# Attention and a mixture of experts on one core: experts behind the first taken in the order of their token counts, with 812 to 768 slots by place

## The chip, the core and the metric

The kernel runs on one core of a Trainium2 chip. The metric is the device time of one execution in microseconds (us). PE is the matrix engine (PEld its weight loads), DVE the vector engine, ACT the scalar engine, POOL the third general engine, which also issues the indirect DMAs, and SP the engine that issues the other DMAs.

## The reference

```python
scores = scale * q @ k.T + bias          # 4 x 8 heads, 768 positions, 64 wide, local window of 96 and 8 global keys
x = softmax(scores) @ v                  # as 3072 tokens of 512
noisy = x @ w_gate + log1p(exp(x @ w_noise)) * noise       # 8 experts
top2 = the two largest of noisy for each token, top2_w their softmax
for e in range(8):
    for k in range(2):
        mask = top2[:, k] == e
        out[mask] += top2_w[mask, k] * (relu(x[mask] @ w1[e]) @ w2[e])     # 512 -> 1024 -> 512
```

With the inputs that the reference draws, the eight experts get 721, 802, 751, 806, 768, 763, 761 and 772 tokens.

## The kernel before

The attention runs in 96 head pairs (24 blocks of 128 tokens). Meanwhile `route` places the tokens of five segments of blocks (`SEG`) in a table `tab` of slots: for each expert 7 columns, 4 of 128 slots (part A, `CA` = 512) and 3 of 100 (part B, `CB` = 300), so `CAP` = 812 for every expert. It is a Python generator: each `yield` is one step, and its caller decides how many steps are written between other work. Its last part makes, for each block, two marks on DVE (L350, L354: tiles `m` and `xg`), and L367 multiplies them on PE into `tab`, in groups of at most three blocks. Instructions run on each engine in the order in which they are written.

The experts come one after another. Their weights are loaded by SP in halves of 1 MB into a ring of three buffers (`load_w`, L130) and each value is split into a high and a low part (`split`: ACT L141, DVE L142). Tokens are gathered by slot (`gather`, L158), transposed on PE (`turn`, L180) and split (ACT L182, DVE L183). `up` multiplies by `w1` for one of 8 pieces `f`, 12 matmuls of 512 columns (part A, c=0) or 300 (part B, c=1), L781; ACT L785 and DVE L786 take the result. `down` (part A, L808) yields a tile of tokens from 24 matmuls of 512 columns. `down_t` (part B, L818) multiplies the other way round, 24 matmuls with the 300 slots as columns, and `back` (L828) transposes its result. `put` scales (ACT L792) and adds the rows into the output by an indirect DMA (POOL L793); its tile `y` has two buffers.

Between the attention and expert 0's first `up`, two routes are unfinished. They are handed to `pending`, and this list says how many steps of each are written ahead of each `up(0, 0, f)`:

```python
steps_of = [24, 0, 8, 100], [0, 25, 0, 0, 0, 26]
```

A branch behind the end computes all experts densely for tokens beyond the slots; it is not entered when no expert has more tokens than `CAP`.

Of the kernel before, what the change touches and what calls it, by code (L numbers as in the profile page):

```python
# [10 lines left out]
F32 = mybir.dt.float32  # L11
# [12 lines left out]
TB, MB = 3, 100  # L24
CA, CB = TA * P, TB * MB
TT = TA + TB
CAP = CA + CB
DUMP = 512


# [1 line left out]
def tile_local_global_attention_then_moe(  # L32
# [13 lines left out]
    nc = tc.nc  # L46
    B, _, _, D, _, HP, Q = q.shape
    H = 2 * HP
    Dm = H * D
# [3 lines left out]
    E, _, F = w1.shape  # L53
    KC, FC = Dm // P, F // P
# [18 lines left out]
    gp = wctx.enter_context(tc.tile_pool(name="gp", bufs=1))  # L73
# [15 lines left out]
    ident = consts.tile([P, P], F32, name="ident")  # L89
# [5 lines left out]
    iota_e = consts.tile([P, SW, E], F32, name="iota_e")  # L95
    carry = consts.tile([P, E], F32, name="carry")
# [17 lines left out]
    raw = {}  # L114
    order = [(x, e, h) for e in range(E) for x in (1, 2) for h in range(2)]
    asked = []

    def load_w(n=1):
        for _ in range(n):
            if len(asked) == len(order):  # L120
                return
            x, e, h = order[len(asked)]
            asked.append(order[len(asked)])
            if x == 1:
                t = wts.tile([P, KC, F // 2], F32, name="raw", tag="raw", bufs=3)
                src = w1[e, :, h * F // 2:(h + 1) * F // 2].rearrange("(k p) f -> p k f", p=P)
            else:
                t = wts.tile([P, FC // 2, Dm], F32, name="raw", tag="raw", bufs=3)
                src = w2[e, h * F // 2:(h + 1) * F // 2].rearrange("(k p) d -> p k d", p=P)
            nc.sync.dma_start(t, src)  # L130
            raw[x, e, h] = t

# [12 lines left out]

    xg = {}

    def rows(e, t):

        m = slice(0, P if t < TA else MB)  # L150
# [12 lines left out]
    def fill(to, e, t):  # L163

        nc.vector.scalar_tensor_tensor(to, tab[:, 0, e, t], 0.0, dump[:, e, t], op0=OP.is_equal, op1=OP.mult)
        nc.vector.tensor_add(to, to, tab[:, 0, e, t])
# [7 lines left out]
    def turn(e, t, ps=None):  # L174
        x = xg.pop((e, t))
        m = x.shape[0]
        c, c0 = (0, t * P) if t < TA else (1, (t - TA) * MB)
# [44 lines left out]
    def route(r):  # L222

        a, z = SEG[r]
        w = z - a
        sh = [P, w, E]
        l = small.tile([P, SW, 2 * E], F32, name=f"l{r % 2}")[:, :w]
        u, t, p, ny, po = (small.tile([P, SW, E], F32, name=f"{x}{r % 2}")[:, :w] for x in ("u", "t", "p", "ny", "po"))
        n = l[:, :, E:]
        nc.vector.tensor_copy(l, lgv[:, r % 2, :w])  # L230
        yield
# [35 lines left out]
        ixf = consts.tile([P, w, 2], F32, name=f"ixf{r}")  # L267
# [13 lines left out]
        we = consts.tile([P, w, 2], F32, name=f"we{r}")  # L281
# [14 lines left out]
        ps = lgp  # L296
# [14 lines left out]
        sl = consts.tile([P, w, 2], F32, name=f"sl{r}")  # L311
# [22 lines left out]
        nc.vector.tensor_sub(fs, fs, row)  # L334
        yield
        bs = [P, w, 2, TT]
        nc.vector.tensor_tensor(band, fs[:, :, :, None].to_broadcast(bs),
# [43 lines left out]
                gather(0, t, DUMP + z * P)  # L381
                yield
        if r == len(SEG) - 1:
            fill(ids, slice(0, E), slice(0, TT))
            nc.vector.tensor_add(tab[:, 1], tab[:, 1], tab[:, 2])  # L385

    kept = []
# [377 lines left out]
    with ExitStack() as mctx:  # L765
# [7 lines left out]
        hl = [mc.tile([P, FC, n], FR, name=f"hl{n}") for n in (CA, CB)]  # L773
        yt = mc.tile([P, KC, CB], F32, name="yt")
        def up(e, c, f, between={}):
            ps = bank("sc" if f % 2 else "at")[:, :hh[c].shape[2]]
            fs = slice(f * P, (f + 1) * P)
            n = 0
            for k in range(KC):
                for w, x in ((w1h, xh), (w1h, xl), (w1l, xh)):  # L780
                    nc.tensor.matmul(ps, w[:, k, fs], x[c][:, k], start=n == 0, stop=n == 3 * KC - 1)  # L781
                    n += 1
                    if n in between:
                        between[n](NT - 1)
            nc.scalar.activation(hh[c][:, f], ps, AF.Relu)  # L785
            nc.vector.scalar_tensor_tensor(hl[c][:, f], ps, 0.0, hh[c][:, f].bitcast(F32),  # L786
                                           op0=OP.max, op1=OP.subtract)

        def put(e, t, ps):
# [20 lines left out]
            put(e, t, ps)  # L810

        def down_t(e, d):
            ps = bank("av")[:, :CB]
            cols = slice(d * P, (d + 1) * P)
            n = 0
            for f in range(FC):
                for w, x in ((w2h, hh), (w2h, hl), (w2l, hh)):
                    nc.tensor.matmul(ps, w[:, f, cols], x[1][:, f], start=n == 0, stop=n == 3 * FC - 1)  # L818
                    n += 1
            if d % 2:  # L820
                nc.vector.tensor_copy(yt[:, d], ps)
            else:
                nc.scalar.activation(yt[:, d], ps, AF.Copy)

        def back(e, t):
            ps = spare_bank()[:MB]
            for d in range(KC):
                nc.tensor.transpose(ps[:, d * P:(d + 1) * P], yt[:, d, t * MB:(t + 1) * MB], ident)  # L828
# [70 lines left out]

    wctx.close()  # L900
    cf = small.tile([1, E + 1], F32, name="cf")
    nc.vector.tensor_scalar(cf[:, :E], carry[:1], float(-CAP), 0.0, op0=OP.add, op1=OP.max)
    nc.vector.reduce_max(cf[:, E:], cf[:, :E], axis=AX.X)
    nc.vector.tensor_copy(more, cf)
    left = nc.values_load(more[0:1, E:E + 1], min_val=0, max_val=N)
    with tc.If(left > 0), tc.tile_pool(name="lc", bufs=1) as lc:
        wov = lc.tile([P, NT, E], F32, name="wov")
        for (a, z), (ixf, sl, we) in zip(SEG, kept):
            w = z - a
            sh = [P, w, E]  # L910
            ov = lc.tile([P, SW, 2], F32, name="ov")[:, :w]
            eq = lc.tile([P, SW, E], F32, name="eq")[:, :w]
            nc.vector.scalar_tensor_tensor(ov, sl, float(CAP), we, op0=OP.is_ge, op1=OP.mult)
# [78 lines left out]
```

## Time and profile before

| | us |
|---|---|
| median of 3 runs | 814.35 |
| lowest and highest | 814.26 and 816.34 |
| profiled execution | 813.31 |
| its span in the trace | 811.5 |

The span is the profiled execution without the 1.8 us that lie around it in its time. PE's busy share counts pipelined matmuls as busy until their modelled ends, so it says that PE hardly waits, and not how fast it works; the pace is read from the distance between starts in the timeline.

### The profile page before, as it was taken

To read this page: it belongs to the slowest core of one execution; us is meant where nothing else is said; L and a number is where in the kernel's file an instruction comes from. 1 tells how busy PE (TensorE), PEld (TensorE's weight loads), DVE (VectorE), ACT (ScalarE), POOL (GpSimd) and SP (SyncE) were. 2 spreads that over 40 slices of the span, in tenths; PEclk is the share of its full clock that TensorE was granted. 3 is DMA by queue.
4 is the path that set the end of the run, shared out by engine and by line. 5 is a ranking of instruction groups with operands and counts; after the bars stand their busy time and mean duration, and the time that the engine had idled before them with its cause. 6 is when DMAs were issued, how large, how long until landed. Compare 5 with 4: busy or idle time off the path is not lost.

```text
span 811.5 us, 14891 instructions
## 1 busy us (share of the span) xinstructions
PE 791.7 (98%) x5697; PEld 701.2 (86%) x5697; DVE 330.5 (41%) x1209; ACT 337.1 (42%) x732; POOL 202.6 (25%) x228
## 2 busy tenths in 40 slices
PE   7999999999699999999999999999999999999995
PEld 6988989888589989898898989898988889898984
DVE  6557575867633434233323423332333334233400
ACT  6778777674223433233323322333333333233301
POOL 2003422451035050313223130504131231212013
PEclk9999999999899999999999999999999999999998
DMA  9889575646065252445344343533443433432015
GB/s 263 245 274 302 188 219 163 209 168 208 18 167 111 55 142 105 65 122 135 76 101 98 100 99 79 145 105 59 124 120 93 101 82 116 99 78 32 1 18 70
DMA packets 61216, 100.46 MB, mean 124 GB/s; under 512 B 7232, under 2 KB 19648, under 8 KB 61136
## 3 DMA queue, kind: packets, MB, share of 16 engines
q1 hardware_dynamic: 47440, 72.79, 28.3%
q0 software_dynamic: 13696, 26.63, 18.1%
q8 instruction: 47, 0.77, 0.4%
q14 instruction: 33, 0.27, 0.1%
HBM read 71.40 MB, written 27.98 MB: 122 GB/s over the span
## 4 chain that ended last, share of the span: by engine, by line
issue 55%; PE 28%; POOL 12%; DVE 3%; DMA 2%; POOLq 0%; ACT 0%; SPq 0%; ACTq 0%
PE av L602 9%; POOL out_dram L793 7%; PE at L582 6%; POOL xg L158 5%; PE sc L554 4%; PE av L808 3%; PE sc L781 1%; PE m L202 1%; DMA out_dram<-y,ids 1%; PE at L781 1%; PE m L210 1%; PE lg L367 1%; PE lg L217 0%; DMA qbuf<-in_q 0%; DMA vs<-in_v 0%
## 5 line engine op out<-in xcount | busy, mean ns | idle before, releaser
L793 POOL DMA_INDIRECT out_dram<-y,ids x56 | 89.3, 1595 | 414.1 <-ACT y L792 409.4
L808 PE MATMUL av<-w2h,hh 128*128 128x512 f32 x256 | 102.8, 402 | 0.0
L808 PE MATMUL av<-w2h,hl 128*128 128x512 f32 x256 | 101.4, 396 | 0.0
L808 PE MATMUL av<-w2l,hh 128*128 128x512 f32 x256 | 101.2, 395 | 0.0
L142 DVE TENSOR_TENSOR w1l<-raw,w1h 128x512 fp32r<-128x512 f32 x56 | 38.3, 689 | 148.2 <-ACT w1h L141 148.2
L781 PE MATMUL sc<-xh,w1h 128*128 128x512 f32 (+1 forms) x256 | 90.7, 354 | 0.0
L781 PE MATMUL at<-xh,w1h 128*128 128x512 f32 (+1 forms) x256 | 89.6, 350 | 0.0
L781 PE MATMUL sc<-xh,w1l 128*128 128x512 f32 (+1 forms) x256 | 89.2, 349 | 0.0
L781 PE MATMUL sc<-xl,w1h 128*128 128x512 f32 (+1 forms) x256 | 89.1, 348 | 0.0
L781 PE MATMUL at<-xl,w1h 128*128 128x512 f32 (+1 forms) x256 | 88.5, 346 | 0.1
L781 PE MATMUL at<-xh,w1l 128*128 128x512 f32 (+1 forms) x256 | 88.5, 346 | 0.0
L786 DVE SCALAR_TENSOR_TENSOR hl<-sc,hh 128x512 fp32r<-128x512 f32 (+1 forms) x64 | 37.2, 581 | 106.4 <-ACT hh L785 106.4
L818 PE MATMUL av<-hh,w2h 128*128 128x300 f32 x256 | 79.0, 309 | 0.0
L785 ACT ACTIVATE hh<-sc 128x512 fp32r<-128x512 f32 (+1 forms) x64 | 32.6, 510 | 108.6 <-PE sc L781 108.6
L158 POOL DMA_INDIRECT xg<-xd,ids x56 | 60.4, 1079 | 66.9 <-DVE tab L385 44.1
L818 PE MATMUL av<-hh,w2l 128*128 128x300 f32 x256 | 77.0, 301 | 0.0
L818 PE MATMUL av<-hl,w2h 128*128 128x300 f32 x256 | 77.0, 301 | 0.0
L570 ACT ACTIVATE a<-ns,mx 128x168 f32<-128x168 f32 (+1 forms) x192 | 71.7, 422 | 7.1 <-POOL a L484 4.2
L792 ACT ACTIVATE y<-av,tab 128x512 f32<-128x512 f32 x28 | 19.3, 688 | 126.2 <-issue 106.4
L602 PE MATMUL av<-vs,at 128*128 128x65 f32 x384 | 70.8, 273 | 0.0
L785 ACT ACTIVATE hh<-at 128x512 fp32r<-128x512 f32 (+1 forms) x64 | 32.7, 511 | 87.7 <-PE at L781 87.6
L584 ACT ACTIVATE at<-at 128x512 f32<-128x512 f32 (+1 forms) x96 | 53.6, 558 | 29.8 <-PE at L582 28.6
(152 smaller groups left out, 1585.7 us busy)
## 6 DMA issues: line engine op xcount, KB each, us to landing
raw<-in_w SPq DMA_DIRECT2D x32, 1024.0 KB, 5.3
out_dram<-zero SPq DMA_DIRECT2D x14, 512.0 KB, 5.7
vs<-in_v SPq DMA_DIRECT2D x24, 260.0 KB, 3.9
qbuf<-in_q SPq DMA_DIRECT2D x24, 256.0 KB, 4.8
xd<-xr SPq DMA_DIRECT2D x24, 256.0 KB, 2.6
ks<-in_k SPq DMA_DIRECT2D x20, 272.0 KB, 3.8
vp<-in_v SPq DMA_DIRECT2D x20, 195.0 KB, 4.7
ks<-in_k SPq DMA_DIRECT2D x4, 464.0 KB
```

Of the source, the lines that this page charges most:

```text
L142: eng.tensor_sub(lo, t, hi.bitcast(F32))
L158: nc.gpsimd.indirect_dma_start(out=xg[e, t], out_offset=None, in_=xd[:n], in_offset=bass.IndirectOffsetOnAxis(ap=r, axis=0), bounds_check= ...
L570: nc.scalar.activation(A[n][:, s, c:c + w], ns[:, s, :w], AF.Exp, bias=mx[:, s:s + 1], scale=-1.0)
L582: nc.tensor.transpose(p4[:, :, c, s * Q:(s + 1) * Q], x[:, s, a:a + P], ident)
L584: nc.scalar.activation(AT[n], ps, AF.Copy)
L602: nc.tensor.matmul(ps[:, h % 4], a[:kk, y * w + c0:y * w + c0 + P], t[:kk, c], start=kk < P or not i, stop=kk == P)
L781: nc.tensor.matmul(ps, w[:, k, fs], x[c][:, k], start=n == 0, stop=n == 3 * KC - 1)
L785: nc.scalar.activation(hh[c][:, f], ps, AF.Relu)
L786: nc.vector.scalar_tensor_tensor(hl[c][:, f], ps, 0.0, hh[c][:, f].bitcast(F32), op0=OP.max, op1=OP.subtract)
L793: ins = nc.gpsimd.indirect_dma_start(out=out, out_offset=bass.IndirectOffsetOnAxis(ap=r, axis=0), in_=y, in_offset=None, bounds_check=N + ...
L808: nc.tensor.matmul(ps, x[0][:, f, cols], w[:, f], start=n == 0, stop=n == 3 * FC - 1)
L818: nc.tensor.matmul(ps, w[:, f, cols], x[1][:, f], start=n == 0, stop=n == 3 * FC - 1)
```

## The change

Expert 0 keeps its place and its 812 slots. When the last route is done, `rank` orders the other seven on DVE by the number of their tokens, largest first, moves the columns of `tab` accordingly and writes the number of the expert at each place into `who`. SP reads `who` to find the weights of a place, so no weights but those of expert 0 can be asked for before; the loads that were due earlier (`held`) are issued then. The slots by place are 812, 812, 804, 792, 780, 768, 768, 768: part B is now cut in tiles of 128, has 300, 300, 292, 280, 268, 256, 256 and 256 columns, and at the last three places its third tile is gone with its `gather`, `turn`, `back` and `put`. `route` loses the three DVE operations (three steps) that turned slots of 100 into rows of 128, and the numbers in `steps_of` are changed. Four small tiles of `route` lose their second buffer. Behind the end, 14 DVE operations where 3 stood put together the number of slots of each expert for the branch.

```diff
+CAPS = [812, 812, 804, 792, 780, 768, 768, 768]
+CB = max(CAPS) - CA
...
     def load_w(n=1):
...
+            if e and not ranked:
+                held[0] += 1
+                continue
...
+                if e not in ranked:
+                    ranked[e] = nc.values_load(who[0:1, e - 1:e], engines=(mybir.EngineType.SP,),
+                                               min_val=1, max_val=E - 1)
+                w = w[ds(ranked[e], 1)].rearrange("e k f -> (e k) f")
...
+    def tiles(e):
+        return -(-CAPS[e] // P)
...
     def gather(e, t, n=DUMP + N):
+        if t >= tiles(e):
+            return
...
+    def rank():
+
+        n = E - 1
+        sq = [P, n, n]
...
+        nc.vector.scalar_tensor_tensor(cnt, iota_e[:, 0, :n], -1.0 / E, carry[:, 1:], op0=OP.mult, op1=OP.add)
+        nc.vector.tensor_tensor(more_, cnt[:, None, :].to_broadcast(sq), cnt[:, :, None].to_broadcast(sq), op=OP.is_gt)
+        nc.vector.tensor_reduce(place, more_, op=OP.add, axis=AX.X)
+
+        nc.vector.tensor_tensor(perm, place[:, None, :].to_broadcast(sq),
+                                iota_e[:, 0, :n][:, :, None].to_broadcast(sq), op=OP.is_equal)
+        nc.vector.tensor_mul(more_, perm, iota_e[:, 0, 1:][:, None, :].to_broadcast(sq))
+        nc.vector.tensor_reduce(cnt, more_, op=OP.add, axis=AX.X)
+        nc.vector.tensor_copy(who, cnt[:1])
+        to = [tab[:, 0], tab[:, 1]]
+        for x in range(2):
+            b = gp.tile([P, Dm], F32, name="xg", bufs=5)[:, :n * n * TT].rearrange("p (r t e) -> p r t e", r=n, t=TT)
+            nc.vector.tensor_tensor(b, perm[:, :, None, :].to_broadcast([P, n, TT, n]),
...
+            nc.vector.tensor_reduce(to[x][:, 1:], b, op=OP.add, axis=AX.X)
+        fill(ids[:, 1:], slice(1, E), slice(0, TT))
...
-        nc.vector.tensor_scalar(fs, sl, float(CA + MB), None, op0=OP.is_ge)
-        yield
-        nc.vector.scalar_tensor_tensor(fs, sl, float(CA + 2 * MB), fs, op0=OP.is_ge, op1=OP.add)
-        yield
-        nc.vector.scalar_tensor_tensor(fs, fs, float(P - MB), sl, op0=OP.mult, op1=OP.add)
-        yield
-        nc.vector.tensor_copy(si, fs)
+        nc.vector.tensor_copy(si, sl)
...
-            ps = bank("sc" if f % 2 else "at")[:, :hh[c].shape[2]]
+            m = CAPS[e] - CA if c else CA
+            ps = bank("sc" if f % 2 else "at")[:, :m]
...
-        steps_of = [24, 0, 8, 100], [0, 25, 0, 0, 0, 26]
+        steps_of = [24, 0, 8, 0, 0, 100], [0, 25, 0, 0, 0, 26]
...
         for t in range(TB):
             gather(0, TA + t)
+        rank()
+        ranked[0] = None
+        load_w(held[0])
         for t in range(TA - 1):
             down(0, t)
```

What stands on PE where expert 0's first `up` begins, before (`ohs` is the segment's one-hot table, `lg` the bank of the routing, `at` that of `up`):

```order
L304 LDWEIGHTS ones
L304 MATMUL lg<-ohs_3529,ones 128x8
L781 MATMUL at<-xh_96,w1h 128x512
L781 MATMUL at<-xl_97,w1h 128x512
L781 MATMUL at<-xh_96,w1l 128x512
L202 MATMUL m<-ident,xr 128x128 x4
```

And the same place of PE in the changed kernel (L410 is the old L367, L825 the old L781):

```order
L354 LDWEIGHTS ones
L354 MATMUL lg<-ohs_3520,ones 128x8
L410 MATMUL lg<-xg,m 128x168 x6
L825 MATMUL at<-xh_98,w1h 128x512
L825 MATMUL at<-xl_99,w1h 128x512
L825 MATMUL at<-xh_98,w1l 128x512
L252 MATMUL m<-ident,xr 128x128 x4
```

The 24 steps now reach three operations further, and the six matmuls of the fourth segment's first three blocks, which stood ahead of `up(0, 0, 2)`, stand ahead of `up(0, 0, 0)`.

What stands on PE ahead of `up(0, 0, 5)` before, where the last segment's counts are summed:

```order
L304 LDWEIGHTS ones
L304 MATMUL lg<-ohs_3757,ones 128x8
L781 MATMUL sc<-xh_96,w1h 128x512
L781 MATMUL sc<-xl_97,w1h 128x512
L781 MATMUL sc<-xh_96,w1l 128x512
```

And the same place of PE in the changed kernel:

```order
L354 LDWEIGHTS ones
L354 MATMUL lg<-ohs_3751,ones 128x8
L410 MATMUL lg<-xg,m 128x168 x6
L825 MATMUL sc<-xh_98,w1h 128x512
L825 MATMUL sc<-xl_99,w1h 128x512
L825 MATMUL sc<-xh_98,w1l 128x512
```

Here the last segment's six matmuls, which stood behind `up(0, 0, 7)`, have come forward to stand directly behind the sums from which DVE makes their marks. The fourth segment's last block (L367 x2) went the other way: from ahead of `up(0, 0, 3)` to just ahead of these sums, behind `up(0, 0, 4)`.

## Rows read from the trace of the kernel before

**Rows 1.** The page, first lines: span, busy time and share of two engines.
```profile
span 811.5 us, 14891 instructions
...
PE 791.7 (98%) x5697; PEld 701.2 (86%) x5697; DVE 330.5 (41%) x1209; ACT 337.1 (42%) x732; POOL 202.6 (25%) x228
```

**Rows 2.** Busy time in stretches: us, PE, PEld, DVE, ACT, POOL, clock, DMA, GB/s.
```profile
203.70:209.90 6.20, 0.00 (x0) 0.00 (x0) 5.80 (x36) 1.69 (x4) 0.00 (x0) 0.84 0.00 1
209.90:214.60 4.70, 4.69 (x12) 3.82 (x13) 1.13 (x3) 0.00 (x0) 0.00 (x0) 0.50 0.02 3
...
264.00:280.00 16.00, 16.00 (x123) 16.00 (x123) 7.12 (x13) 6.07 (x13) 0.00 (x0) 1.00 0.23 66
```

**Rows 3.** Timeline of PE, an up step of 512 columns, then one of 300.
```profile
300.47 0.39 PE L781 MATMUL sc<-xh,w1h 128*128 128x512 f32 x1
...
303.19 0.30 PE L781 MATMUL at<-xh,w1h 128*128 128x300 f32 x1
...
304.84 0.30 PE L781 MATMUL sc<-xh,w1h 128*128 128x300 f32 x1
```

**Rows 4.** Timeline of PE, transposes of a turn and of a back between matmuls.
```profile
343.89 0.51 PE L180 MATMUL m<-ident,xg 100*128 100x100 f32 x4
344.18 0.39 PE L818 MATMUL av<-hh,w2h 128*128 128x300 f32 x1
...
357.67 0.60 PE L828 MATMUL lg<-ident,yt 128*100 128x128 f32 x4
358.02 0.47 PE L781 MATMUL sc<-xh,w1h 128*128 128x512 f32 x1
358.34 0.39 PE L781 MATMUL sc<-xl,w1h 128*128 128x512 f32 x1
```

**Rows 5.** Timeline of PE in the attention: two pairs of L602.
```profile
188.10 0.39 PE L602 MATMUL av<-vs,at 128*128 128x65 f32 x2
188.32 0.39 PE L602 MATMUL av<-vp,at 104*128 104x65 f32 x2
```

**Rows 6.** Timeline of PE around the first up steps of expert 0.
```profile
192.85 0.47 PE L781 MATMUL at<-xh,w1h 128*128 128x512 f32 x1
...
200.12 0.80 PE L367 MATMUL lg<-xg,m 128*128 128x168 f32 x6
...
209.91 0.75 PE L367 MATMUL lg<-xg,m 128*128 128x168 f32 x2 [6.21 <-DVE xg L354]
...
227.12 0.42 PE L808 MATMUL av<-w2h,hh 128*128 128x512 f32 x1
```

**Rows 7.** Timeline of DVE, routing of the last two segments, and after.
```profile
193.99 0.18 DVE L307 TENSOR_TENSOR po<-lg,carry 128x32 f32<-128x32 f32 x1
...
198.99 0.20 DVE L230 COPY l<-lg 128x48 f32<-128x48 f32 x1
...
201.66 0.17 DVE L235 TENSOR_SCALAR t<-u 128x24 f32<-128x24 f32 x1
...
207.70 0.68 DVE L786 SCALAR_TENSOR_TENSOR hl<-sc,hh 128x512 fp32r<-128x512 f32 x1
...
220.02 0.17 DVE L307 TENSOR_TENSOR po<-lg,carry 128x24 f32<-128x24 f32 x1
...
224.97 0.69 DVE L786 SCALAR_TENSOR_TENSOR hl<-sc,hh 128x512 fp32r<-128x512 f32 x1
...
245.32 0.57 DVE L183 TENSOR_TENSOR xl<-m,xh 128x400 fp32r<-128x400 f32 x1 [15.19 <-ACT xh L182]
...
270.37 1.28 DVE L142 TENSOR_TENSOR w1l<-raw,w1h 128x512 fp32r<-128x512 f32 x2
```

**Rows 8.** Timeline of PE and ACT at the end; the page, DMA issues (to landing).
```profile
802.80 0.40 PE L808 MATMUL av<-w2h,hl 128*128 128x512 f32 x1
...
804.17 0.69 ACT L792 ACTIVATE y<-av,tab 128x512 f32<-128x512 f32 x1 [3.57 <-DMA out_dram<-y,ids]
...
raw<-in_w SPq DMA_DIRECT2D x32, 1024.0 KB, 5.3
```

More of the change, by code (lines that the diff above doesn't have):

```diff
@@ L23 @@
 TA = 4
-TB, MB = 3, 100
-CA, CB = TA * P, TB * MB
+TB = 3
+CA = TA * P
 TT = TA + TB
-CAP = CA + CB
+CAPS = [812, 812, 804, 792, 780, 768, 768, 768]
+CB = max(CAPS) - CA
 DUMP = 512
@@ L105, in tile_local_global_attention_then_moe @@
     ids = consts.tile([P, E, TT], I32, name="ids")
+    perm = consts.tile([P, E - 1, E - 1], F32, name="perm")
+    who = consts.tile([1, E - 1], I32, name="who")
     more = consts.tile([1, E + 1], I32, name="more")
@@ L116, in tile_local_global_attention_then_moe @@
     asked = []
+    ranked, held = {}, [0]
     def load_w(n=1):
@@ L161, in gather, with fill @@
             bounds_check=n - 1, oob_is_err=False)
-    def fill(to, e, t):
-        nc.vector.scalar_tensor_tensor(to, tab[:, 0, e, t], 0.0, dump[:, e, t], op0=OP.is_equal, op1=OP.mult)
-        nc.vector.tensor_add(to, to, tab[:, 0, e, t])
+    def fill(to, e, t, of=None):
+        of = tab[:, 0] if of is None else of
+        nc.vector.scalar_tensor_tensor(to, of[:, e, t], 0.0, dump[:, e, t], op0=OP.is_equal, op1=OP.mult)
+        nc.vector.tensor_add(to, to, of[:, e, t])
+    def rank():
+        n = E - 1
+        sq = [P, n, n]
+        cnt = small.tile([P, n], F32, name="cnt")
+        more_ = gp.tile([P, Dm], F32, name="xg", bufs=5)[:, :n * n].rearrange("p (r e) -> p r e", r=n)
+        place = small.tile([P, n], F32, name="place")
+        nc.vector.scalar_tensor_tensor(cnt, iota_e[:, 0, :n], -1.0 / E, carry[:, 1:], op0=OP.mult, op1=OP.add)
[10 more added lines that the diff above has]
+            nc.vector.tensor_tensor(b, perm[:, :, None, :].to_broadcast([P, n, TT, n]),
+                                    tab[:, x, 1:].rearrange("p e t -> p t e")[:, None].to_broadcast([P, n, TT, n]),
+                                    op=OP.mult)
+            nc.vector.tensor_reduce(to[x][:, 1:], b, op=OP.add, axis=AX.X)
+        fill(ids[:, 1:], slice(1, E), slice(0, TT))
     spare = [0]
@@ L174, in turn @@
     def turn(e, t, ps=None):
+        if t >= tiles(e):
+            return
         x = xg.pop((e, t))
         m = x.shape[0]
-        c, c0 = (0, t * P) if t < TA else (1, (t - TA) * MB)
+        c, c0 = (0, t * P) if t < TA else (1, (t - TA) * P)
         ps = (spare_bank() if ps is None else ps)[:, :KC * m].rearrange("p (k t) -> p k t", k=KC)
@@ L227, in route @@
         l = small.tile([P, SW, 2 * E], F32, name=f"l{r % 2}")[:, :w]
-        u, t, p, ny, po = (small.tile([P, SW, E], F32, name=f"{x}{r % 2}")[:, :w] for x in ("u", "t", "p", "ny", "po"))
+        u, t, p, ny, po = (small.tile([P, SW, E], F32, name=x)[:, :w] for x in ("u", "t", "p", "ny", f"po{r % 2}"))
         n = l[:, :, E:]
@@ L333, in route @@
         yield
-        nc.vector.tensor_sub(fs, fs, row)
+        nc.vector.tensor_sub(fs, sl, row)
         yield
@@ L383, in route @@
         if r == len(SEG) - 1:
-            fill(ids, slice(0, E), slice(0, TT))
+            fill(ids[:, 0, TA:], 0, slice(TA, TT))
             nc.vector.tensor_add(tab[:, 1], tab[:, 1], tab[:, 2])
@@ L780, in up @@
                 for w, x in ((w1h, xh), (w1h, xl), (w1l, xh)):
-                    nc.tensor.matmul(ps, w[:, k, fs], x[c][:, k], start=n == 0, stop=n == 3 * KC - 1)
+                    nc.tensor.matmul(ps, w[:, k, fs], x[c][:, k, :m], start=n == 0, stop=n == 3 * KC - 1)
                     n += 1
@@ L784, in up @@
                         between[n](NT - 1)
[L785 to L786 removed]
+            nc.scalar.activation(hh[c][:, f, :m], ps, AF.Relu)
+            nc.vector.scalar_tensor_tensor(hl[c][:, f, :m], ps, 0.0, hh[c][:, f, :m].bitcast(F32),
                                            op0=OP.max, op1=OP.subtract)
@@ L812, in down_t @@
         def down_t(e, d):
-            ps = bank("av")[:, :CB]
+            m = CAPS[e] - CA
+            ps = bank("av")[:, :m]
             cols = slice(d * P, (d + 1) * P)
@@ L817, in down_t @@
                 for w, x in ((w2h, hh), (w2h, hl), (w2l, hh)):
-                    nc.tensor.matmul(ps, w[:, f, cols], x[1][:, f], start=n == 0, stop=n == 3 * FC - 1)
+                    nc.tensor.matmul(ps, w[:, f, cols], x[1][:, f, :m], start=n == 0, stop=n == 3 * FC - 1)
                     n += 1
             if d % 2:
-                nc.vector.tensor_copy(yt[:, d], ps)
+                nc.vector.tensor_copy(yt[:, d, :m], ps)
             else:
-                nc.scalar.activation(yt[:, d], ps, AF.Copy)
+                nc.scalar.activation(yt[:, d, :m], ps, AF.Copy)
         def back(e, t):
-            ps = spare_bank()[:MB]
+            m = min(P, CAPS[e] - CA - t * P)
+            if m <= 0:
+                return
+            ps = spare_bank()[:m]
             for d in range(KC):
-                nc.tensor.transpose(ps[:, d * P:(d + 1) * P], yt[:, d, t * MB:(t + 1) * MB], ident)
+                nc.tensor.transpose(ps[:, d * P:(d + 1) * P], yt[:, d, t * P:t * P + m], ident)
             put(e, TA + t, ps)
-        steps_of = [24, 0, 8, 100], [0, 25, 0, 0, 0, 26]
+        steps_of = [24, 0, 8, 0, 0, 100], [0, 25, 0, 0, 0, 26]
         def ahead(g):
@@ L901, in tile_local_global_attention_then_moe @@
     cf = small.tile([1, E + 1], F32, name="cf")
-    nc.vector.tensor_scalar(cf[:, :E], carry[:1], float(-CAP), 0.0, op0=OP.add, op1=OP.max)
+    past = ctx.enter_context(tc.tile_pool(name="past", bufs=1))
+    cap = past.tile([P, E], F32, name="cap")
+    capr = past.tile([P, E - 1], F32, name="capr")
+    capm = past.tile([P, E - 1, E - 1], F32, name="capm")
+    for x, n in enumerate(CAPS):
+        nc.vector.memset(capr[:, x - 1:x] if x else cap[:, :1], float(n))
+    nc.vector.tensor_mul(capm, perm.rearrange("p r e -> p e r"), capr[:, None, :].to_broadcast([P, E - 1, E - 1]))
+    nc.vector.tensor_reduce(cap[:, 1:], capm, op=OP.add, axis=AX.X)
+    nc.vector.tensor_sub(cf[:, :E], carry[:1], cap[:1])
+    nc.vector.tensor_scalar(cf[:, :E], cf[:, :E], 0.0, None, op0=OP.max)
     nc.vector.reduce_max(cf[:, E:], cf[:, :E], axis=AX.X)
@@ L912, in tile_local_global_attention_then_moe @@
             eq = lc.tile([P, SW, E], F32, name="eq")[:, :w]
-            nc.vector.scalar_tensor_tensor(ov, sl, float(CAP), we, op0=OP.is_ge, op1=OP.mult)
+            for j in range(2):
+                nc.vector.tensor_tensor(eq, iota_e[:, :w], ixf[:, :, j:j + 1].to_broadcast(sh), op=OP.is_equal)
+                nc.vector.tensor_mul(eq, eq, cap[:, None, :].to_broadcast(sh))
+                nc.vector.tensor_reduce(ov[:, :, j], eq, op=OP.add, axis=AX.X)
+            nc.vector.tensor_tensor(ov, sl, ov, op=OP.is_ge)
+            nc.vector.tensor_mul(ov, ov, we)
             for j in range(2):
```

10 lines of the change are left out of this document (7 added, 3 removed).

## The prediction

> **What bounds the kernel now.** I read the page first: PE is busy for 98% of the span, no other engine for half of it [rows 1]. So behind the attention the time is the sum of what PE has to do, plus the places where PE waits. The timeline of PE gives the pace, by the distance between starts: an `up` step of 12 matmuls with 512 columns takes 303.19 - 300.47 = 2.72 us, one with 300 columns takes 304.84 - 303.19 = 1.65 us [rows 3], that is 227 and 137.5 ns for a matmul. The difference is 89 ns for 212 columns: 0.42 ns for a column, the pace of the 2.4 GHz level, with about the same 13 ns on top of both. So at these widths the columns are what costs, and fewer columns are fewer nanoseconds.
>
> The view of idle times of PE has one large entry behind the start: L367 waits 6.21 us for a mark of DVE, at 203.7 to 209.9 [rows 6]. It costs more than itself: the granted clock falls inside this idle time and is 0.50 (the 1.2 GHz level) for the next 4.7 us [rows 2], in which PE gets half done, a further 2.2 us or so. Whoever moves the routing's operations moves this wait, so I followed the order of both kernels there.
>
> **The change, part by part.**
>
> *Columns.* Part B loses 0, 0, 8, 20, 32, 44, 44 and 44 columns, together 192. Each expert has 8 x 12 matmuls of part B in `up` and 4 x 24 in `down_t`, together 192. 192 x 192 x 0.42 ns = 15.5 us off PE's path. No row of before shows 256 columns. The nearest rows bound it: if the pace were set by something that does not shrink, the gain would be 0; what speaks for the whole gain is that pairs of L602, which load 128 weight columns for every matmul as these do, start 0.11 us apart (two in 188.32 - 188.10 = 0.22) [rows 5], and 137.5 - 44 x 0.42 = 119 ns is still above that. I take 15.5.
>
> *Transposes.* A group of four in `turn` takes 344.18 - 343.89 = 0.29 us, one in `back` 358.02 - 357.67 = 0.35, and the matmul behind it starts its successor 0.09 later than usual (0.32 in place of 0.23) [rows 4]. Three of each are gone: 3 x 0.38 + 3 x 0.44 = 2.5. Two groups of each `turn` now move 128 columns in place of 100, up to the 0.35 of `back`: 14 x 0.06 = 0.8 back. Net 1.7 (2.5 if width costs nothing). The `gather`s, `put`s and conversions of the lost tiles lie on POOL, ACT and DVE, which have room.
>
> *The end.* The last `y` starts at 804.17 because its buffer waits for an earlier addition to land (3.57 us), while the last matmul ends at 802.80 + 0.40 = 803.20 [rows 8]. With one `back` fewer, the buffer's earlier user lies one `put` further back. Gain 0.9 (0 to 1).
>
> *The routing, first place.* The six matmuls that stood ahead of `up(0, 0, 2)` and found their marks ready (no idle time at 200.12) now stand ahead of `up(0, 0, 0)`, which started at 192.85 [rows 6]. DVE begins this part at 193.99 and has finished the three blocks' marks at 198.99 [rows 7]; three operations less, at about 0.2 us each, make it 198.4. PE follows the three blocks as they come, so `up(0, 0, 0)` starts at 198.7: 5.2 us of new idle time, and the 0.64 us of the six matmuls, which only move. All that stands behind on PE comes later by it, the last block's gate first, and with that DVE's chain for the last segment.
>
> *Second place.* At full clock the first two steps last 7.3 us (192.85 to 200.12, with the gate in the first) and three more 8.2, so PE passes `up(0, 0, 4)` at 214.2. DVE has the last segment's gate by 203, then a conversion pair, the chain of 6.04 us (201.66 to 207.70) [rows 7], another pair and the marks of the fourth segment's last block, 213.7 in all. So the old wait of 6.21 us is gone: that block is ready when PE comes. Then PE sums the last segment's counts (214.6 with both), and behind the sums now stand the six matmuls of its marks. DVE first has conversions to do, to about 217, then the run that lasted 224.97 - 220.02 = 4.95 us [rows 7], 4.35 without the three operations: 221.3. PE goes on at 221.6, idle for some 6.4 us. Before, three `up` steps lay in between and PE found these marks ready.
>
> *The sum of both places.* Three steps more (8.2) bring `down(0, 0)` to 229.8, where it was 227.12 [rows 6]: 2.7 us lost if the clock stays up, though the old wait and its slow clock are gone. The second wait is as long as the old one, which brought the clock down; I count its 2.2 us. The first is shorter and has three short bursts in its last part; it may or may not. So 4.9 with one fall, 7.1 with two; I take 6.0 lost, with ends at 2.7 and 8.
>
> *`rank`.* 13 operations on DVE: at 0.17 to 0.69 us (the smallest and the 512-wide in [rows 7]) between 2 and 9 us, about 4 by their widths of 7 to 343. They lie in the 15.19 us in which DVE waits before 245.32 [rows 7], while PE is in three `down`s. Behind them on DVE stand the `turn`s of part B, and on POOL the gathers of expert 1 wait for the new `ids`; both are due only after those `down`s. Nothing, or its own length if that cover went.
>
> *Weights.* Three loads of expert 1, which were issued at their turn in the queue before, now wait for `who`, some 5 us behind the start of `down(0, 0)`: about 235. With 5.3 us to land each [rows 8] and one behind the other they are there by 252; the first is split at 270.37 [rows 7] (276 by the new clock of events). So 20 us of cover remain. The register load ahead of each later expert has no row; its lower end is 0, its upper the load it delays, 5.3 us, and each half is asked for long before its first split. Nothing. The additional DVE operations behind the end of the program lie under the last `down`s: nothing, or some 14 x 0.2 = 3 us without that cover.
>
> The sum: -15.5 - 1.7 - 0.9 + 6.0 = -12.1. From the profiled execution's own 813.31 this gives 801.2. The median of the runs is 1.04 above that execution, so I forecast 814.35 - 12.1 = 802.3 as a median.
>
> **Rivals.**
> *The routing costs less:* if DVE reaches the second place earlier, or neither idle time brings the clock down, the two places cost 2.7 or less: 799.0, down to 796.3. For it: each wait is broken by bursts of PE as block follows block. Against it: the old wait of about this length did bring it down.
>
> *The weight loads set the pace in part B.* In the stretch from 264 to 280, which is all 300 columns wide, PEld is busy for 16.00 of 16.00 us [rows 2]. If that is a bound, narrower matmuls start no closer than 137.5 ns, and only 1.7 + 0.9 are gained against 6.0 lost: 817.8, slower than before. It decides once less than 3.4 of the 15.5 us remain, that is, at a floor of 133 ns or more for 256 columns. Against it speak the 0.11 us of [rows 5] and the equal 13 ns at both widths [rows 3].
> The Trainium skill (Perfetto Trace Analysis, Identifying the Most-Contended Engine) says that headroom of the matrix engine is judged by the busy share of LDWEIGHTS and not by that of the matmuls. By that rule part B has no headroom and the result would be this rival's; the pace by columns at 300 and 512 in this trace speaks against it, and no row at 256 columns decides it.
>
> *The weights of expert 1 come late,* if `who` or its reading takes far longer than an operation of its size: 20 us are covered, then each us costs one; 12 us beyond would be needed to lose the gain. 802 to 814.
>
> *Slots overflow.* The counts are 721, and in order 806, 802, 772, 768, 763, 761, 751 against 812, and 812, 804, 792, 780, 768, 768, 768; the closest is 802 of 804. One token above would enter the dense branch, which loads 4 MB per expert and goes over 24 blocks; four loads of 5.3 us and 24 rounds of a load and a store would cost above 100 us. The reference's own counts speak against it, unless the chip decides some near ties otherwise.
>
> **How the numbers follow.** I give the forecast 0.74, the cheaper routing 0.16, the weight loads as bound 0.04, late weights 0.04, overflow 0.02. What a measurement here can tell from no change is about 0.3%, 2.4 us. Faster is the forecast and the cheaper routing, 0.90; late weights I count as no change, 0.04; slower is the rest, 0.06. The forecast alone goes from 799.5 to 805.5 (the routing at 2.7 to 8, the transposes and the end at their bounds). The range takes in most of the cheaper routing, and above it a column that pays only three quarters (3.9 us) or a longer second wait: 796.5 to 807.5.
>
> **What would show it.** PE's L825 and L863 at 256 columns starting 119 ns apart in the last three experts, and these experts' stretches shorter by some 4 us each; idle times of PE for a mark of DVE ahead of the first `up` and ahead of `up(0, 0, 5)`, about 5 and 6 us, and a granted clock of 0.50 behind at least one; none where the old one was; `down(0, 0)` at 230 to 235. Wrong would be: starts at 256 columns as far apart as at 300, a wait of PE or ACT for `raw` in expert 1, or a trace in which the clock does not fall.

## The result and the profile after

Compared on the same chip, the changed kernel takes 805.39 us (median of 4 runs, 805.13 to 807.52), the kernel before 815.06 (814.26 to 816.34): ratio 0.9897, 95% interval 0.9881 to 0.9914, so 1.0% faster. Forecast were 802.3 (796.5 to 807.5). The profiled execution took 805.52.

The page of the changed kernel, span and first line of busy times (as [rows 1]):

```profile
span 803.7 us, 14896 instructions
...
PE 778.4 (97%) x5673; PEld 686.4 (85%) x5673; DVE 330.7 (41%) x1215; ACT 332.5 (41%) x726; POOL 192.3 (24%) x222
```

The view of waits for PE (engine, tile, line, what it waited for: us in total, times, longest):

```profile
PE lg L410 <- DVE xg L397: 6.0, 2, 3.5
...
PE lg L350 <- DVE tab L413: 2.6, 1, 2.6
```

The old 6.21 us [rows 6] are gone, but three waits with 8.6 us in all have come. The timeline of PE says where (start, duration, tile, idle time ahead):

```profile
193.59 0.24 PE L354 MATMUL lg<-ohs,ones 128*128 128x8 bf16 x4
197.35 2.51 PE L410 MATMUL lg<-xg,m 128*128 128x168 f32 x6 [3.53 <-DVE xg L397]
199.66 0.70 PE L825 MATMUL at<-xh,w1h 128*128 128x512 f32 x1
...
216.37 0.35 PE L410 MATMUL lg<-xg,m 128*128 128x168 f32 x2
219.28 0.19 PE L350 MATMUL lg<-ohs,upper 128*128 128x8 bf16 x2 [2.57 <-DVE tab L413]
...
222.17 2.51 PE L410 MATMUL lg<-xg,m 128*128 128x168 f32 x6 [2.52 <-DVE xg L397]
224.48 0.70 PE L825 MATMUL sc<-xh,w1h 128*128 128x512 f32 x1
...
234.09 0.40 PE L852 MATMUL av<-w2h,hh 128*128 128x512 f32 x1
```

The view counts a wait only up to the first block's marks. At each place the six matmuls then follow the blocks as they come and stretch over 2.3 us (197.35 to 199.66, 222.17 to 224.48).

The windows of the changed kernel (columns as in [rows 2]) around the two places, and in a part B of 256 columns:

```profile
196.80:203.50 6.70, 5.89 (x21) 4.29 (x24) 2.50 (x12) 0.60 (x1) 0.00 (x0) 0.50 1.01 373
...
220.70:227.40 6.70, 4.98 (x13) 3.96 (x14) 3.31 (x16) 0.00 (x0) 0.00 (x0) 0.50 0.00 0
...
680.00:686.00 6.00, 6.00 (x53) 6.00 (x52) 3.33 (x8) 2.87 (x7) 0.00 (x0) 1.00 0.47 171
```

Both places bring the granted clock down to 0.50. The pace of `up` with 256 columns, from the timeline of PE; an up step lasts 607.42 - 606.01 = 1.41 us, 117.5 ns a matmul:

```profile
606.01 0.28 PE L825 MATMUL at<-xh,w1h 128*128 128x256 f32 x1
...
607.42 0.28 PE L825 MATMUL sc<-xh,w1h 128*128 128x256 f32 x1
```

And the end, from the timeline of all engines (as [rows 8]); the span ends at 803.7:

```profile
792.31 0.40 PE L852 MATMUL av<-w2h,hl 128*128 128x512 f32 x1
792.80 0.69 ACT L836 ACTIVATE y<-av,tab 128x512 f32<-128x512 f32 x1 [4.91 <-PEq L966]
793.76 1.57 POOL L837 DMA_INDIRECT out_dram<-y,ids  x1 [4.03 <-ACT y L836]
```

In the kernel before, the last addition's issue stands 6.4 us ahead of the end of the span, here 10.0; its row of before, from the timeline of POOL:

```profile
805.15 1.59 POOL L793 DMA_INDIRECT out_dram<-y,ids  x1 [2.66 <-ACT y L792]
```

The spans of the two profiled executions differ by 7.8 us. By stretches of PE's timeline:

| stretch | before | after | change | forecast |
|---|---|---|---|---|
| start to the last sums ahead of the first `up` | 192.75 | 193.59 | +0.8 | 0 |
| from there to `down(0, 0)` (routing) | 34.4 | 40.5 | +6.1 | +6.0 |
| to the end of the last matmul (columns, transposes) | 576.1 | 558.6 | -17.5 | -17.2 |
| to the end of the span | 8.3 | 11.0 | +2.7 | -0.9 |

So three terms came as forecast in sum, and the end went the other way by 3.6 us. The +0.8 is not laid to the change. PE's rows are alike in both up to 8.73; then its pairs of transposes run slower for longer in this execution (first row of before, then of after, timeline of PE):

```profile
10.05 0.44 PE L582 MATMUL at<-ident,a 128*128 128x128 f32 x2
```

```profile
10.06 0.69 PE L625 MATMUL at<-ident,a 128*128 128x128 f32 x2
```

At 11.43 and 12.54 they begin the next scores. In the fourteen traces the granted clock comes up at 9.5 to 16.5 us, and two of them (e1 and x2 of the experiments) show a fall of it in the attention; the sums in the table stand at 192.75 to 198.05. Single times of one kernel lie up to 6 us apart (the kernel before from 815.40 to 821.44 on one chip). From `down(0, 0)` to the last matmul runs with the same slots repeat within 0.2 us, and the routing's stretch of runs with the same order within 0.5 (w1_widths is 1.1 longer than its like, with a longer fall of the clock), so the experiments are read by these stretches first.

### The profile page after: what moved, and what is told of

Same layout as the page of the kernel before. It is cut to its first block, busy times and chain, and to the rows that moved or that the text cites. A ratio compares the mean times of both kernels' runs of the same rounds, so it can differ in the third digit from the quotient of the medians.

```text
span 803.7 us, 14896 instructions
## 1 busy us (share of the span) xinstructions
PE 778.4 (97%) x5673; PEld 686.4 (85%) x5673; DVE 330.7 (41%) x1215; ACT 332.5 (41%) x726; POOL 192.3 (24%) x222
## 4 chain that ended last, share of the span: by engine, by line
issue 53%; PE 29%; POOL 11%; DVE 3%; DMA 2%; POOLq 0%; ACT 0%; SPq 0%; ACTq 0%
PE av L645 9%; POOL out_dram L837 7%; PE at L625 6%; PE sc L597 4%; POOL xg L180 4%; PE av L852 3%; DMA out_dram<-y,ids 1%; PE m L252 1%; PE at L825 1%; PE m L260 1%; PE sc L825 1%; PE lg L410 1%; PE lg L267 1%; DMA qbuf<-in_q 0%; DVE hl L830 0%
## 5 line engine op out<-in xcount | busy, mean ns | idle before, releaser
L825 PE MATMUL at<-xh,w1h 128*128 128x512 f32 (+5 forms) x256 | 88.9, 347 | 0.0
L825 PE MATMUL sc<-xh,w1h 128*128 128x512 f32 (+5 forms) x256 | 88.7, 347 | 0.0
L825 PE MATMUL sc<-xh,w1l 128*128 128x512 f32 (+5 forms) x256 | 87.6, 342 | 0.0
L825 PE MATMUL at<-xh,w1l 128*128 128x512 f32 (+5 forms) x256 | 87.6, 342 | 0.0
L825 PE MATMUL sc<-xl,w1h 128*128 128x512 f32 (+5 forms) x256 | 87.4, 342 | 0.0
L825 PE MATMUL at<-xl,w1h 128*128 128x512 f32 (+5 forms) x256 | 87.4, 341 | 0.0
L830 DVE SCALAR_TENSOR_TENSOR hl<-sc,hh 128x512 fp32r<-128x512 f32 (+5 forms) x64 | 36.3, 568 | 103.8 <-ACT hh L829 103.8
L863 PE MATMUL av<-hh,w2h 128*128 128x256 f32 (+4 forms) x256 | 76.1, 297 | 0.0
L863 PE MATMUL av<-hh,w2l 128*128 128x256 f32 (+4 forms) x256 | 74.1, 290 | 0.0
L863 PE MATMUL av<-hl,w2h 128*128 128x256 f32 (+4 forms) x256 | 74.1, 290 | 0.0
```

Of the source, the lines that this page charges most:

```text
L825: nc.tensor.matmul(ps, w[:, k, fs], x[c][:, k, :m], start=n == 0, stop=n == 3 * KC - 1)
L830: nc.vector.scalar_tensor_tensor(hl[c][:, f, :m], ps, 0.0, hh[c][:, f, :m].bitcast(F32), op0=OP.max, op1=OP.subtract)
L863: nc.tensor.matmul(ps, w[:, f, cols], x[1][:, f, :m], start=n == 0, stop=n == 3 * FC - 1)
```

## The experiments

**Is it the routing's places that cost 6 us?** Rival: the loss comes from other edits of the routing (the four tiles of `route` that lost their second buffer). Two runs of the changed kernel with other places, and two of the kernel before with the order changed alone.

```diff
-        steps_of = [24, 0, 8, 0, 0, 100], [0, 25, 0, 0, 0, 26]   # changed kernel
+        steps_of = [21, 0, 8, 100], [0, 25, 0, 0, 0, 23]         # e1_old_places
+        steps_of = [21, 0, 8, 0, 0, 100], [0, 25, 0, 0, 0, 23]   # e2_old_places_late_block
-        steps_of = [24, 0, 8, 100], [0, 25, 0, 0, 0, 26]         # kernel before
+        steps_of = [24, 0, 8, 0, 0, 100], [0, 25, 0, 0, 0, 26]   # e3_before_late_block
+        steps_of = [27, 0, 8, 0, 0, 100], [0, 25, 0, 0, 0, 29]   # e4_before_new_places
```

> The changed kernel with the routing's operations put back to their old places on PE (21, 0, 8, 100 and 0, 25, 0, 0, 0, 23 steps), all else as changed. If the new places cost the 6 us between the attention and the first down, the old idle time of some 6 us with one fall of the clock is back, the stretch from the end of the attention to down(0, 0) is 34.3 us in place of 40.4, and the time is 805.4 - 6.1 = 799.3 (798.3 to 800.3). If the loss comes from the other edits (four small tiles of the routing without their second buffer, the fewer operations), the stretch stays near 40 and the time near 805. In both cases the last matmul stands 11.0 us ahead of the end of the span.

Measured: 801.74 (798.88 to 803.98), ratio to the kernel before 0.9809 (0.9777 to 0.9841). The median is above the range expected: in the profiled execution (803.46) the granted clock is 0.50 from 186 to 192 us, in the attention, and the other long one has the same mean clock (0.986, against 0.990 in the two short ones). Timeline of PE:

```profile
198.05 0.24 PE L354 MATMUL lg<-ohs,ones 128*128 128x8 bf16 x4
...
214.61 0.75 PE L410 MATMUL lg<-xg,m 128*128 128x168 f32 x2 [5.60 <-DVE xg L397]
...
231.47 0.80 PE L410 MATMUL lg<-xg,m 128*128 128x168 f32 x6
232.11 0.42 PE L852 MATMUL av<-w2h,hh 128*128 128x512 f32 x1
```

The stretch is 232.11 - 198.05 = 34.1 us, the old one, with the old wait and no other. The last matmul ends 11.0 us ahead of the end of the span, as expected.

> The kernel before with the order on PE of the changed kernel (27, 0, 8, 0, 0, 100 and 0, 25, 0, 0, 0, 29 steps), nothing else. If the new places alone cost the 6 us, 814.4 + 6.1 and up to 1.2 for the six routing operations that this kernel still has: 821 (820 to 822), with two idle times ahead of the first up and ahead of up(0, 0, 5). If the other edits cost it, 814 to 815.

Measured: 822.18 (821.04 to 822.78), 0.2 above the range expected, ratio 1.0071 (1.0054 to 1.0088). The timeline of PE shows the waits of the changed kernel in the body of the old one:

```profile
193.74 0.24 PE L304 MATMUL lg<-ohs,ones 128*128 128x8 bf16 x4
198.11 2.51 PE L367 MATMUL lg<-xg,m 128*128 128x168 f32 x6 [4.13 <-DVE xg L354]
...
219.94 0.19 PE L300 MATMUL lg<-ohs,upper 128*128 128x8 bf16 x2 [2.57 <-DVE tab L370]
...
223.42 2.51 PE L367 MATMUL lg<-xg,m 128*128 128x168 f32 x6 [3.12 <-DVE xg L354]
...
235.01 0.40 PE L808 MATMUL av<-w2h,hh 128*128 128x512 f32 x1
```

41.3 us in place of 34.4: the places alone cost it. The rival falls.

> As the run before, but the one block's entries (two matmuls) stand behind up(0, 0, 4) as in the changed kernel: 21, 0, 8, 0, 0, 100 and 0, 25, 0, 0, 0, 23 steps. PE comes there some 16.1 us behind the end of the attention, DVE's mark was ready 17.1 us behind it, so of the old 6.2 us at most 1 is left, no fall of the clock (2.2); the sums behind it may wait for the addition into the table as in the changed kernel (2.6). Stretch 34.3 - 8.4 + 1 + 2.6 = 29.5 us, time 794.5 (791 to 797). If the wait only moves with the matmuls, because DVE's marks then stand behind its other work, the stretch is 34 and the time 799.

Measured: 796.55 (796.29 to 801.48), ratio 0.9775 (0.9741 to 0.9809). The stretch is 30.8 us, 1.3 more than expected: a fall of the clock behind the wait (0.50 for 3.4 us) was not in the sum. The view of waits of PE holds the sums' wait for the table and almost nothing at the moved block:

```profile
PE lg L350 <- DVE tab L413: 2.9, 1, 2.9
...
PE lg L410 <- DVE xg L397: 0.2, 1, 0.2
```

> The kernel before with that one move alone (24, 0, 8, 0, 0, 100 and 0, 25, 0, 0, 0, 26 steps). By the same sum 814.4 - 4.8 = 809.6 (807 to 811.5); if the wait only moves, 814. The last matmul stands 8.3 us ahead of the end of the span, as before, if the code behind the end sets that distance.

Measured: 812.83 (811.46 to 816.55), ratio 0.9972 (0.9948 to 0.9996); the stretch is 31.2 us, 3.1 less, where 4.8 were expected. The same 2.9 us at the sums stand there, and the same short fall of the clock, which the sum had left out. So moving the block is good; moving the other two groups with it is what cost.

**Can the wait at the sums go too?** The sums write the bank from which DVE adds the block's entries into `tab`, so they wait for that addition. One `up` step between them:

```diff
-        steps_of = [21, 0, 8, 0, 0, 100], [0, 25, 0, 0, 0, 23]
+        steps_of = [21, 0, 8, 0, 0, 100], [0, 25, 0, 0, 0, 0, 23]
```

> The kernel of e2_old_places_late_block with the sums of the last segment's counts one up step later (21, 0, 8, 0, 0, 100 and 0, 25, 0, 0, 0, 0, 23 steps). There PE waits 2.9 us at the sums, behind the one block's two matmuls, for DVE's addition into the table, and a short fall of the clock costs 1.7. If an up step between the two covers the addition, both are gone; DVE then has two up steps (5.45 us) for its run of 4.4 us and the conversions, so the last six matmuls may wait 0 to 1.5. Stretch from the end of the attention to down(0, 0) 31.1 - 4.6 + 0.7 = 27.2, time 796.4 - 3.9 = 792.5 (791 to 794). If DVE is the bound of this stretch, the wait moves to the last six matmuls: 796.

Measured: 791.34 (790.88 to 793.28), ratio 0.9717 (0.9700 to 0.9735): 2.8% below the kernel before, and below the changed one. Timeline of PE, and the window from the first `up` to `down(0, 0)`:

```profile
209.86 0.59 PE L410 MATMUL lg<-xg,m 128*128 128x168 f32 x2 [0.18 <-DVE xg L397]
...
213.49 0.22 PE L354 MATMUL lg<-ohs,ones 128*128 128x8 bf16 x3
...
219.15 0.80 PE L410 MATMUL lg<-xg,m 128*128 128x168 f32 x6
219.79 0.42 PE L852 MATMUL av<-w2h,hh 128*128 128x512 f32 x1
```

```profile
193.40:219.79 26.39, 26.01 (x139) 20.53 (x136) 23.45 (x104) 8.71 (x18) 0.00 (x0) 1.00 0.30 110
```

The stretch is 26.5 us (27.2 expected), PE is idle for 0.4 of it and the clock stays at 1.00. DVE is busy for 23.5 of 26.4 us there, so little room is left on it.

**What makes the end longer?** The distance from the last matmul to the end of the span was 8.3 to 8.5 us in the kernels with the old body and 11.0 to 11.2 in those with the new one. Three suspects: the code behind the end, the place of POOL's instructions (POOL executes 479 in the kernel before, 462 in the changed one), the spacing of the last additions. Then two more, the number of indirect copies and SP's registers.

```diff
+    nc.vector.tensor_scalar(cf[:, :E], carry[:1], float(-CAP), 0.0, op0=OP.add, op1=OP.max)   # t1_old_tail: in place of cap, and in the branch
...
+            if e == 3:                              # t2_pool_17
+                for _ in range(17):
+                    nc.gpsimd.memset(pad, 0.0)
...
-                elif j in (KC, KC + 1, KC + 2):
-                    back(e, j - KC)
+                elif j in (KC + 1, KC + 2):         # x1_backs_later
+                    back(e, j - KC - 1)
+                elif j in (KC, KC + 1):             # x2_before_backs_earlier
+                    for t in ([0, 1], [2])[j - KC]:
+                        back(e, t)
```

> The kernel of e2_old_places_late_block with the end of the kernel before: one threshold of 812 in place of the slots by place (so tokens between a place's slots and 812 would be left out; there are none with these inputs), 3 operations of DVE behind the last down_t in place of 14, and the shorter code of the branch. The last matmul stood 8.3 to 8.5 us ahead of the end of the span in the three kernels with this end, 11.0 to 11.2 in the three with the new one. If the code at the end makes the difference, it is 8.4 here and the time 796.4 - 2.7 = 793.7. If it is where POOL's instructions lie (POOL executes 17 fewer in the changed kernel, and more instruction packets are loaded behind its jump), or the spacing of the last additions, it stays 11.1 and the time 796.4.

Measured: 795.84 (795.57 to 798.42); the end stays at 11.1 us. Not the code.

> The kernel of e2_old_places_late_block with 17 memsets of one column on POOL inside expert 3, where POOL has room, so that POOL executes as many instructions as in the kernel before and its last ones lie where they lay. If the place of POOL's instructions makes the end longer, the distance from the last matmul to the end goes from 11.2 to about 8.4 us; if the code of the end or the spacing of the last additions does, it stays 11.1.

Measured: 795.51 in one run; the end stays at 11.0 us. Not the place of POOL's instructions.

> The kernel of v6_sums_later with the last expert's two backs each one down later, so that down 3's y takes the buffer of down 2's, as in the kernel before. In all kernels with the changed body the last addition is issued 1.05 us behind the last matmul, 5.6 us behind the addition ahead of it, and the end of the span comes 10.0 us behind that issue; in the three with the old body it is issued 1.95 behind the last matmul, 4.2 behind the addition ahead of it, and the end comes 6.4 behind it. If the spacing of the last additions sets this, the last y waits about 1 us here and the end comes 8.4 us behind the last matmul in place of 11.2: time 791.3 - 2.8 = 788.5. If something else sets it (the number of indirect copies, 106 in place of 112), the last y's wait is added: 12.1 us, time 792.3.

Measured: 794.50 (793.69 to 799.97), ratio 0.9715 (0.9682 to 0.9747). The last addition is issued 1.5 us behind the last matmul and the end comes 9.9 us behind that issue. Not the spacing.

> The kernel before with the last expert's backs brought forward (two behind the first down, one behind the second), so that the last y need not wait for a buffer. If the spacing of the last additions sets the distance from the last issue to the end, it is 10.0 us here and the end comes 11 us behind the last matmul in place of 8.3: 814.9 + 2.7 = 817.6. If not, the distance stays 6.4, the last y starts 0.9 earlier, and the time is 814.0.

Measured: 817.03 (815.43 to 821.05), ratio 0.9998 (0.9973 to 1.0022): the kernel before takes 817.01 on that chip, so this time does not speak for the spacing, though it lies near the 817.6. The end comes 6.2 us behind the last issue. The spacing falls from this side too.

The records of POOL in the traces say where these microseconds lie. The last of its instructions that takes long is a `DRAIN` behind the end of the program. With the old body it begins 0.9 us behind the last issue and takes 4.4 to 4.6 us. With the new one it begins 3.1 to 3.2 us behind it and takes 5.7 to 6.2; in t2_pool_17 (and in c1_all_812 below), where POOL executes 479 instructions again, it begins at 0.9 us as before, but takes 8.1 (8.3). So the place of POOL's instructions moves the start of the drain by 2.2 us and not its end, 5.4 to 5.5 us behind the last issue with the old body and 8.8 to 9.4 with the new one. Nor does the landing of the copies set it: their last packet ends 4.2 to 4.7 us behind that issue in all fourteen traces.

**Columns, copies, rank.**

```diff
-CAPS = [812, 812, 804, 792, 780, 768, 768, 768]
+CAPS = [812] * 8                                   # c1_all_812
...
+PLACE = [0, 3, 1, 7, 4, 5, 6, 2]                   # s1_static_places
...
-        rank()
-        ranked[0] = None
-        load_w(held[0])
+        fill(ids[:, 1:], slice(1, E), slice(0, TT))
```

> The kernel of v6_sums_later with 812 slots at every place, so rank, who and the order of the experts stay, and the 192 columns and the three tiles are back. By the traces the stretch from down(0, 0) to the last matmul goes from 558.6 to 576 us or a little over (the wider groups of transposes stay): time 791.3 + 17.5 to 18.5 = 809 to 810 if the end keeps its 11.1 us. If the number of indirect copies (112 again in place of 106) sets the distance from the last matmul to the end, this falls to some 8.4 us and the time is 806 to 807.

Measured: 812.24 (811.09 to 814.00), ratio 0.9980 (0.9968 to 0.9991), 2 us above the 809 to 810 expected. From `down(0, 0)` to the last matmul 579.0 us, 20.4 more than in v6_sums_later. The end of the span, 810.5, comes 10.1 us behind the last issue, so the number of copies is not it. Timeline of PE, the narrow third tile of a `turn` with its neighbours, and of POOL the last issue; then the neighbours of the tile of 100 in [rows 4], from the kernel before:

```profile
344.56 0.30 PE L863 MATMUL av<-hh,w2l 128*128 128x300 f32 x1
344.79 0.44 PE L230 MATMUL m<-ident,xg 44*128 44x44 f32 x4
345.16 0.41 PE L863 MATMUL av<-hh,w2h 128*128 128x300 f32 x1
345.41 0.31 PE L863 MATMUL av<-hl,w2h 128*128 128x300 f32 x1
...
800.44 1.56 POOL L837 DMA_INDIRECT out_dram<-y,ids  x1 [2.48 <-ACT y L836]
```

```profile
343.75 0.30 PE L818 MATMUL av<-hh,w2l 128*128 128x300 f32 x1
...
344.40 0.30 PE L818 MATMUL av<-hl,w2h 128*128 128x300 f32 x1
```

> The kernel of v6_sums_later without rank and who: the experts' order for these inputs is written out in the program, the weights are asked for at their old turns without a register, and the end is that of the kernel before (one threshold). If rank and the late weights are hidden, as forecast, the stretch from down(0, 0) to the last matmul stays 558.6. If SP's reading of registers in the loop of experts is behind the longer end, this goes from 11.2 to 8.4 us and the time to 788.5; if the number of copies is, the end stays 11.2 and the time 791.3. If rank and the late weights cost something after all, the stretch is shorter by that.

Measured: 791.40 (790.36 to 791.62), ratio 0.9713 (0.9692 to 0.9734), with 558.8 us from `down(0, 0)` to the last matmul: within 0.2 us of the same with `rank`. The end stays at 11.1 us, so SP's registers are not it either.

**Where does the pace stop following the columns?**

```diff
+CAPS = [812, 768, 736, 704, 672, 640, 608, 576]
```

> The kernel of t1_old_tail with 812, 768, 736, 704, 672, 640, 608, 576 slots by place, so that part B is 300, 256, 224, 192, 160, 128, 96 and 64 columns wide; the tokens beyond these slots are left out of the sum. Read is only the distance between matmuls of up in part B. If columns alone set it, it falls by 0.42 to 0.45 ns a column all the way: 103 ns at 224, 89 at 192, 74 at 160, 60 at 128, 46 at 96, 31 at 64. If the weight load of 128 columns sets a floor, it stops falling at a width below 256; the pairs of the attention at 110 ns for 65 columns would put that near 240.

Measured (803.62 in one run): 137.5 ns a matmul fell to 117.8 at 256 columns, and then to 111.6 at 224, 111.4 at 192, 111.3 at 160 and 111.1 at 128. Timeline of PE, 224 columns and 128, ten matmuls apart:

```profile
373.98 0.27 PE L826 MATMUL at<-xh,w1l 128*128 128x224 f32 x1
...
375.10 0.28 PE L826 MATMUL sc<-xh,w1h 128*128 128x224 f32 x1
...
581.23 0.28 PE L826 MATMUL at<-xh,w1l 128*128 128x128 f32 x1
...
582.35 0.28 PE L826 MATMUL sc<-xh,w1h 128*128 128x128 f32 x1
```

Each pace is the length of the eight up steps by their 96 matmuls. So there is a floor of 111 ns, reached between 256 and 224 columns. That the weight load sets it is not shown, since no run changes the weights of these matmuls. Other rows bear on it: the `bf16` sums of the routing load 128 weight columns too and start 0.025 us apart (at 193.38, 193.41 and 193.43 in the changed kernel), and the groups of `back` there take 0.35 us with 12, 24, 36, 44 and 128 weight columns alike. So the number of weight columns alone does not make the floor. Below 128 columns something else comes on top; the windows of this kernel, 128 columns, then 96 twice, then 64:

```profile
581.50:591.50 10.00, 10.00 (x92) 10.00 (x91) 5.32 (x12) 4.38 (x12) 0.00 (x0) 1.00 0.31 105
...
649.50:654.50 5.00, 5.00 (x47) 5.00 (x46) 2.66 (x6) 2.34 (x6) 0.00 (x0) 1.00 0.34 103
655.00:664.00 9.00, 9.00 (x44) 9.00 (x43) 2.42 (x6) 1.78 (x5) 0.00 (x0) 0.50 0.11 40
...
745.50:765.50 20.00, 20.00 (x96) 20.00 (x95) 1.14 (x3) 1.14 (x4) 0.00 (x0) 0.50 0.00 0
```

With 96 columns PE ran 5 us at full clock, without any idle time and with starts 112 ns apart, and then the clock fell to 0.50 and the starts went to 213 ns.

## Why the prediction was right, and where it was not

The direction and the range held; the sum of -12.1 was 2 to 4 us too good (-9.7 by the medians, -7.8 by the profiled executions, of which +0.8 lies ahead of the first `up`). The largest term and the routing were right in their mechanism. That columns and transposes together came within 0.3 us of the forecast is in part luck: the first gave more than forecast, the second less.

- *Columns*, -15.5: c1_all_812 against v6_sums_later gives 8.42 us for `up`'s half (13.24 us in each of seven experts against 84.26 in all), 16.8 for both if `down_t`'s half is like it. The pace at 256 columns is 117.8 ns where 119 was worked out. Right in its mechanism, 1.3 us too small.
- *The weight loads as bound*: against this rival the prediction set the pairs at 0.11 us. They were the right row: the floor is 111 ns. The Trainium skill (Perfetto Trace Analysis, Identifying the Most-Contended Engine) judges headroom by MFU (the share of the peak arithmetic rate) and by the busy share of LDWEIGHTS. That share was full at 300 columns [rows 2] and is full at 256 (6.00 of 6.00 above), yet the pace fell by 20 ns between them, and by 6 more to 224; only below that does the share tell of a bound here. A full share does not say how far away the floor is; two widths of the same matmul do.
- *Transposes*, -1.7: -0.7. Of the 20.4 us of c1_all_812, 3.6 are left for the three tiles, more than the 2.5 worked out. But the same stretch is 579.0 there and 576.1 in the kernel before: tiles of 128, 128 and 44 cost 2.9, not 0.8. The forecast left the third, narrow tile at the price of one of 100 columns. Its group takes 345.16 - 344.79 = 0.37 us, as much as one of 128 and more than one of 100 (0.29, [rows 4]), and its neighbours are slower too: from the matmul ahead of it to the second behind it 345.41 - 344.56 = 0.85 us pass, with 100 columns 344.40 - 343.75 = 0.65, and with 128 columns 0.72 (337.04 to 337.76 in c1_all_812). By these numbers eight narrow tiles cost 1.6 and sixteen wide ones 1.1, so 2.7 of the 2.9 (an estimate).
- *Routing*, +6.0: +6.1, nearly by the pieces forecast. From the sums to `up(0, 0, 0)` 199.66 - 193.59 = 6.07 us pass, where 198.7 - 192.75 = 5.95 were forecast; the 3.5 us in the view of waits are only the part ahead of the first marks. The second place took 224.48 - 216.37 = 8.1 us, where 221.6 - 214.2 = 7.4 were forecast, but of these 2.6 lie ahead of the sums, which wait for the addition of the block's entries, a wait that I had not seen. Both falls of the clock came. The steps between the places took 16.7 us in place of 15.5 and those behind them 9.6 in place of 8.2, so the two falls cost about 2.6 us (an estimate): each less than the 2.2 that I had counted for a fall, both together less than the 3.3 in the sum. e1 and e4 show that the places cost the 6 us; the other edits of the routing cost nothing that the stretch shows (34.1 us in e1, 34.4 before).
- *`rank` and weights*, nothing: s1_static_places shows both together. `rank` runs from 237.5 to 242.1 and leaves DVE 10.8 us idle before its next operation.
- *The end*, -0.9: the step that failed. The last `y` did start as forecast, 0.1 us behind the last matmul in place of 1.0. But I counted the end from there as unchanged, and behind the last issue it is 10.0 us long where it was 6.4 (805.15 to 811.5), so the term came as +2.7. POOL's instructions end last. In all ten profiles of the new body the distance is 9.7 to 10.2, in the four of the old one 6.2 to 6.4. It is not the code behind the end, nor the place of POOL's instructions, the spacing or number of copies, nor `rank` and registers. What the new bodies still share is above all tiles of 128 rows in place of 100 (112 copies, gathers and additions, make 11,776 packets on the queue of the indirect copies in c1_all_812, 13,696 in the kernel before), four small tiles with one buffer, three DVE operations fewer in `route`, and `ids` filled in two parts. None was tried apart; the cause stays open.

## What to carry to other kernels

A change to a generator's number of steps moves every operation behind it. Here the list kept three steps too many for each route: with three off and nothing else (e2 against the changed kernel) the routing's stretch is 30.8 us in place of 40.5, and the time 0.9775 of the kernel before in place of 0.9897; one more up step ahead of the sums makes it 0.9717 (v6). Price what a part costs behind the last matmul as well, on every engine, down to the end of the span. And measure the pace at two widths before making matmuls narrower: it follows the columns only down to a floor.

## What the runs showed of the hardware

- In w1_widths the matmuls of part B (float32, 128 weight columns each) start no closer than 111 to 112 ns on average, from 224 columns down to 64, as long as the clock is at 1.00. The `bf16` sums with 128 weight columns start 25 ns apart.
- The granted clock fell to 0.50 with PE busy throughout, in stretches of 96 and 64 columns, and matmuls of 96 columns then started 0.21 us apart.
- A group of four transposes of 44 columns takes 0.37 us, as long as one of 128 (0.36) and longer than one of 100 (0.29); with its neighbours it cost 0.2 us more than one of 100.
- POOL's closing `DRAIN` ended 5.4 to 5.5 us behind the last indirect addition with one body and 8.8 to 9.4 with the other, and the program 6.2 to 6.4 and 9.7 to 10.2, whatever code stood behind the end and wherever POOL's instructions lay; the last packet had landed at 4.2 to 4.7 in both.
